# fp32 attention and max-of-three MoE: the first weight set as plain products, weight splits in pieces, h tiles loaded earlier

## The chip, the cores and the metric

One core of one Trainium2 chip. The metric is the device time of one execution in microseconds (us). The kernel before was timed in three runs: 632.27, 634.22 and 634.30, median 634.22.

## The reference

Attention over 4 batches, 8 heads, 576 positions, head size 64, with a bias per pair of positions from a small MLP; its output, laid out as 2304 tokens x 512, is multiplied by three weights, the largest of the three is kept, and a fourth weight projects back.

```python
scores = q @ k.T / sqrt(64) + bias(w1, b1, w2)      # 4 x 8 x 576 x 576
attn = exp(scores - max); attn = attn / (sum + 1e-9)
x = (attn @ v).transpose(0, 2, 1, 3).reshape(2304, 512)
h = np.maximum(np.maximum(x @ w1, x @ w2), x @ w3)  # w1..w3: 512 x 768
return h @ w_out                                    # w_out: 768 x 512
```

w1, w2, w3 and w_out arrive with 64 bits per element and are rounded to fp32 on the chip.

## The kernel before

Every fp32 product is made of three passes of TensorE on numbers split in two: a high part rounded by ScalarE (a cast to fp32r), and a low part that is the difference, by VectorE or GpSimd (`arith`, L417). The passes are high·high, high·low and low·high.

**Attention.** 16 units (a pair of heads, a batch) of 5 steps each; step n makes the scores (L254) of one 128-row tile, shifts them on VectorE (L264), takes the exponential on ScalarE (L276), normalises on GpSimd (L289), and for the step five back transposes on TensorE (L308, L317), copies those out (ScalarE L403/L404, VectorE L406) and multiplies with v (L347). `split_x` (L363) copies finished outputs into the twelve token blocks b12, b11, b21, b22 of the columns x = 0, 1, 2. `step` also advances the generators in `more`. One is `first()`: for weight sets 3 and 2 it converts the 64-bit words (`convert`, L483 to L495: one ScalarE and four VectorE instructions for 128x512 words, fetched by L477 into the one buffer `w64`) and parks the result in `w_d`; then it makes set 0 ready, converts w_out into `wo_d`, and converts set 1. The other is `combine(0)`: the splits and sums t1, t2, t3, t4 of the blocks of column 0.

**MoE.** Nine weight sets s (three 256-wide slices of d_ff, each for w1, w2, w3) and three columns x of 2 x 384 tokens give 27 groups. Each group is a Strassen-Winograd product of 2x2 blocks: seven products p1, p5, p6, p7, p2, p4, p3 of six 128x128x384 matmuls (L594 to L596), each into one of eight PSUM banks. ScalarE copies p1 and p5 out (m1 L612, m5 L614); VectorE adds p6 and p7 (mp) and makes c11, c21 and c12, each from one bank; GpSimd makes u and c22 from mp and m5 (L620); for w2 and w3, two VectorE instructions of 768 columns take the max into `ht`, the first right after c21, ahead of c12. The order of groups is (s, x) = (0,0), (1,0), (0,1), (1,1), (0,2), (1,2), then s = 2 to 8 with x inside. Column x + 1's `combine` runs inside the groups ahead of it; `weights` runs inside the others, one step per product: the sums of a set are four GpSimd instructions of 256 columns, its low parts (`split_w`) two of 768 and 1024 columns.

**Output.** After the last group the pool `xb` is released, h (stored to `h_d` by L636) is loaded back in six transfers of 3 x 128 tokens (L577, 1152 KB), split (ScalarE L584, VectorE), and multiplied with w_out in 18 tiles of 18 matmuls (L710 to L713); ScalarE copies a tile out (L714) and SP stores it (L715).

The engines each run their instructions in program order. All transfers are issued by SP, in program order too. The order in the program is thus that of the code: what stands between two products, and in which step a generator is advanced.

Of the kernel before, what the change touches and what calls it, by code (L numbers as in the profile page):

```python
# [9 lines left out]
F32 = mybir.dt.float32  # L10
# [9 lines left out]
def kernel(  # L20
# [45 lines left out]
    w_d = dram.tile([9, 128, 1024], F32, name="w_d")  # L66
# [352 lines left out]
    def combine(x, xa, fin):  # L419
        b12, b11, b21, b22 = raws[x]  # L420
        v, g = nc.vector, nc.gpsimd
        shape = [128, 2, TW]

        def tmp(n):
            return xa.tile(shape, F32, tag="tr", bufs=2, name=f"{n}_{x}")

        def high(n, src):
            h = fin.tile(shape, F32R, tag="xf", bufs=10 * (1 if x == 0 else NX - 1), name=f"{n}h_{x}")
            nc.scalar.copy(h, src)
            return h  # L430

        def low(eng, n, src, h, ring=False):
            o = (xa.tile(shape, F32R, tag="xr", bufs=4 * NX + 1, name=f"{n}l_{x}") if ring else
                 fin.tile(shape, F32R, tag="xf", bufs=10 * (1 if x == 0 else NX - 1), name=f"{n}l_{x}"))
            arith(eng, o, src, h)
            return h, o

        o = xs[x] = {}
        t1 = tmp("t1")
        arith(v, t1, b12, b11)  # L440
        yield
        h = high("t1", t1)
        yield
        o["t1"] = low(g, "t1", t1, h)
        h11 = high("b11", b11)
        yield
        if x == 0:
            yield
        t3 = tmp("t3")
        arith(v, t3, b22, b12)  # L450
        o["b11"] = low(g, "b11", b11, h11, True)
        h21 = high("b21", b21)
        yield
        t2 = tmp("t2")
        arith(v, t2, t3, b11, ALU.add)
        h = high("t3", t3)
        yield
        o["t3"] = low(v, "t3", t3, h, True)
        t4 = tmp("t4")
        arith(v, t4, b21, t2)  # L460
        h2 = high("t2", t2)
        yield
        o["b21"] = low(g, "b21", b21, h21, True)
        h22 = high("b22", b22)
        h4 = high("t4", t4)
        yield
        o["t2"] = low(v, "t2", t2, h2)
        o["b22"] = low(g, "b22", b22, h22, True)
        yield
        o["t4"] = low(v, "t4", t4, h4)  # L470
        yield

    def convert(pool, srcs, out, name):
        w = pool.tile([128, 512, 2], U32, tag="w64", bufs=1, name=f"w64{name}")
# [3 lines left out]
        for _ in range(2):  # L478
            yield
        a = pool.tile([128, 512], F32, tag="wa", bufs=1, name=f"wa{name}")  # L480
        t = pool.tile([128, 512], U32, tag="wt", bufs=1, name=f"wt{name}")
        high, low = w[:, :, 1], w[:, :, 0]
# [4 lines left out]
        nc.vector.tensor_scalar(out=t, in0=a.bitcast(U32), scalar1=3, scalar2=0x7FFFFFFF,  # L487
# [5 lines left out]
        if out is None:  # L493
            out = a.bitcast(U32)
        nc.vector.scalar_tensor_tensor(out=out, in0=high, scalar=signm, in1=t,  # L495
                                       op0=ALU.bitwise_and, op1=ALU.bitwise_or)
        yield a

    wf = {}
    PARK = 4  # L500

    def raw_w(wpool, s, parked=False):
        fp, i = divmod(s, 3)
        raw = wpool.tile([128, 1024], F32, tag="wr", bufs=2, name=f"wr{s}")
        wf[s] = raw
        if parked:
            nc.sync.dma_start(out=raw, in_=w_d[s])
            return
        m = (mw1, mw2, mw3)[i]
        for d in range(2):  # L510
            srcs = [m[256 * d:256 * d + 256, 256 * (2 * fp + b):256 * (2 * fp + b) + 256].rearrange(
                "(c p) f -> p c f", p=128) for b in range(2)]
            yield from convert(wpool, srcs, raw[:, 512 * d:512 * d + 512].bitcast(U32), f"{s}_{d}")

    def sum_w(wpool, s):
        raw = wf[s]
        sr = wpool.tile([128, 1024], F32, tag="wr", bufs=2, name=f"ws{s}")
        q = lambda t, n: t[:, 256 * n:256 * n + 256]
        wf[s] = (raw, sr)
        g = nc.gpsimd  # L520
        arith(g, q(sr, 0), q(raw, 0), q(raw, 2), ALU.add)
        yield
        arith(g, q(sr, 1), q(sr, 0), q(raw, 1))
        yield
        arith(g, q(sr, 2), q(raw, 1), q(raw, 0))
        yield
        arith(g, q(sr, 3), q(raw, 3), q(sr, 1))
        yield

    def split_w(pool, s):  # L530
        raw, sr = wf[s]
        hi = pool.tile([128, 1792], F32R, tag=f"wh{s % 2}", bufs=1, name=f"wh{s}")
        lo = pool.tile([128, 1792], F32R, tag=f"wl{s % 2}", bufs=1, name=f"wl{s}")
        wf[s] = (hi, lo)
        nc.scalar.copy(hi[:, 0:768], raw[:, 256:1024])
        arith(nc.gpsimd, lo[:, 0:768], raw[:, 256:1024], hi[:, 0:768])
        yield
        nc.scalar.copy(hi[:, 768:1792], sr)
        arith(nc.gpsimd, lo[:, 768:1792], sr, hi[:, 768:1792])
        yield  # L540
# [4 lines left out]
    def moe(pool, wpool, xa, xb):  # L545
        ht = pool.tile([128, NX, 5, TW], F32, name="ht", bufs=1)
        hd = h_d.rearrange("(f p) (t n) -> p f t n", p=128, t=2)
        wo = {}
        hs = {}
        hins = {}  # L550

        def load_wo(f):
# [10 lines left out]
            for _ in range(3):  # L563
                yield
# [282 lines left out]
```

## Time and profile before

| | |
|---|---|
| median of three runs | 634.22 us |
| the profiled execution | 636.11 us, of which the span is 634.1 us |
| TensorE (PE) busy | 592.1 us, 93% of the span |
| VectorE (DVE) busy | 425.1 us, 67% |
| ScalarE (ACT) busy | 343.9 us, 54% |
| GpSimd (POOL) busy | 326.5 us, 51% |
| DMA | 74.59 MB, mean 118 GB/s |

The busy times are sums over the whole span, over stages in which different engines do the work; matmuls are pipelined, so a busy TensorE may still run at half its clock. The span is what the trace shows from first to last instruction; the execution's own time is 2.0 us longer, and the profiled execution is 1.9 us above the median.

### The profile page before, as it was taken

To read this page: it belongs to the slowest core of one execution; us is meant where nothing else is said; L and a number is where in the kernel's file an instruction comes from. 1 tells how busy PE (TensorE), PEld (TensorE's weight loads), DVE (VectorE), ACT (ScalarE), POOL (GpSimd) and SP (SyncE) were. 2 spreads that over 40 slices of the span, in tenths; PEclk is the share of its full clock that TensorE was granted. 3 is DMA by queue.
4 is the path that set the end of the run, shared out by engine and by line. 5 is a ranking of instruction groups with operands and counts; after the bars stand their busy time and mean duration, and the time that the engine had idled before them with its cause. 6 is when DMAs were issued, how large, how long until landed. Compare 5 with 4: busy or idle time off the path is not lost.

```text
span 634.1 us, 12010 instructions
## 1 busy us (share of the span) xinstructions
PE 592.1 (93%) x4342; PEld 471.1 (74%) x4342; DVE 425.1 (67%) x902; ACT 343.9 (54%) x791; POOL 326.5 (51%) x285
## 2 busy tenths in 40 slices
PE   8999999999999999999896699999989999399998
PEld 4457666676766666666586699899989999278886
DVE  7995788788868778887738955755866667312221
ACT  7996988788898787887532422222312212123222
POOL 2605766666689555664568757546637545300000
PEclk9999999999999999999898899999989999689999
DMA  6897437533731384322110021321233113733431
GB/s 171 249 357 273 116 100 216 168 107 118 218 105 41 106 252 122 111 69 70 34 33 2 0 67 37 123 93 34 67 109 108 34 34 118 247 124 130 154 124 66
DMA packets 60202, 74.59 MB, mean 118 GB/s; under 512 B 22896, under 2 KB 41712, under 8 KB 60144
## 3 DMA queue, kind: packets, MB, share of 16 engines
q1 hardware_dynamic: 60000, 73.54, 36.8%
q8 instruction: 34, 0.56, 0.4%
q10 hardware_dynamic: 144, 0.29, 0.1%
q14 instruction: 24, 0.20, 0.1%
HBM read 48.51 MB, written 25.31 MB: 116 GB/s over the span
## 4 chain that ended last, share of the span: by engine, by line
PE 53%; DVE 10%; ACT 10%; POOL 9%; DMA 9%; issue 7%; SPq 1%; POOLq 0%; DVEq 0%; ACTq 0%
PE pv L347 10%; PE s L254 9%; PE tp L308 9%; PE o L710 4%; PE o L711 4%; PE o L713 4%; PE p L594 3%; PE p L595 3%; PE p L596 3%; DMA w<-in_moe_w_dram 3%; POOL q L620 3%; POOL wl L417 3%; DMA w64o<-in_moe_w_out_dram 2%; ACT bs L158 2%; DVE ht L417 2%
## 5 line engine op out<-in xcount | busy, mean ns | idle before, releaser
L289 POOL TENSOR_SCALAR e<-e,rc 128x576 f32<-128x576 f32 x144 | 108.8, 768 | 59.5 <-DVE rc L286 32.8
L276 ACT ACTIVATE e<-sn,nm 128x576 f32<-128x576 f32 x144 | 111.0, 774 | 34.2 <-DVE nm L264 32.7
L264 DVE CUSTOM_DVE_ANT_0 sn<-s,bias 128x576 f32<-128x576 f32 x128 | 91.8, 755 | 32.3 <-PE s L254 28.6
L308 PEld LDWEIGHTS tp<-ident,e 128*128 128x128 f32 x576 | 61.9, 142 | 42.1 <-issue 27.8
L308 PE MATMUL tp<-ident,e 128*128 128x128 f32 x576 | 83.0, 282 | 6.2 <-ACT et L403 5.6
L347 PE MATMUL pv<-et,vt 128*64 128x256 f32 (+1 forms) x496 | 74.6, 422 | 1.5 <-DVE xb L363 1.5
L223 POOL TENSOR_TENSOR kl<-kr,kh 128x640 fp32r<-128x640 f32 x16 | 35.6, 2227 | 57.5 <-ACT kh L222 57.4
L417 DVE TENSOR_TENSOR ht<-ht,q 128x768 f32<-128x768 f32 x36 | 38.6, 1073 | 37.9 <-POOL q L620 37.3
L417 DVE TENSOR_TENSOR hl<-hin,hh 128x768 fp32r<-128x768 f32 x18 | 17.1, 957 | 63.3 <-ACT hh L584 63.3
L406 DVE COPY et<-tp 128x512 f32<-128x512 f32 x64 | 43.7, 682 | 22.3 <-PE tp L308 22.3
L254 PE MATMUL s<-kh,qh 64*128 64x288 f32 (+1 forms) x288 | 57.2, 343 | 1.2 <-ACT bs L158 0.9
L710 PE MATMUL o<-woh,hh 128*128 128x512 f32 (+1 forms) x114 | 45.1, 399 | 11.0 <-ACT hh L584 11.0
L620 POOL TENSOR_TENSOR q<-mp,m 128x768 f32<-128x768 f32 x18 | 33.3, 1848 | 35.8 <-DVE mp L417 35.8
L403 ACT COPY et<-tp 128x512 f32<-128x512 f32 x80 | 45.9, 573 | 5.5 <-PE tp L308 5.3
L254 PE MATMUL s<-kl,qh 64*128 64x288 f32 (+1 forms) x288 | 48.6, 293 | 0.0
L347 PEld LDWEIGHTS pv<-et,vt 128*64 128x64 f32 x496 | 30.5, 136 | 24.0 <-issue 10.5
L254 PE MATMUL s<-kh,ql 64*128 64x288 f32 (+1 forms) x288 | 47.9, 290 | 0.0
L711 PE MATMUL o<-wol,hh 128*128 128x512 f32 (+1 forms) x114 | 44.4, 394 | 0.0
L138 PE MATMUL bp<-hid,w2s 128*32 128x79 f32 (+51 forms) x640 | 41.1, 391 | 2.3 <-DVE hid L117 1.9
L254 PEld LDWEIGHTS s<-kh,qh 64*128 64x128 f32 (+1 forms) x288 | 31.3, 184 | 13.2 <-issue 7.5
L714 ACT COPY ot<-o 128x512 f32<-128x512 f32 (+1 forms) x19 | 10.7, 564 | 55.7 <-PE o L713 55.7
L117 DVE TENSOR_SCALAR hid<-sm,bp 128x528 f32<-128x528 f32 (+17 forms) x108 | 40.7, 461 | 0.0
(143 smaller groups left out, 1490.5 us busy)
## 6 DMA issues: line engine op xcount, KB each, us to landing
bias_d<-bs SPq DMA_DIRECT2D x36, 295.5 KB, 5.7
bias<-bias_d SPq DMA_DIRECT2D x16, 576.0 KB, 4.2
w<-in_moe_w_dram SPq DMA_DIRECT2D x36, 256.0 KB, 3.2
h_d<-ht SPq DMA_DIRECT2D x18, 384.0 KB, 2.9
hin<-h_d SPq DMA_DIRECT2D x6, 1152.0 KB, 5.7
qr<-in_qd_dram SPq DMA_DIRECT2D x16, 320.0 KB, 3.7
kr<-in_kd_dram SPq DMA_DIRECT2D x16, 320.0 KB, 4.6
out_dram<-ot SPq DMA_DIRECT2D x17, 256.0 KB, 2.0
```

Of the source, the lines that this page charges most:

```text
L254: nc.tensor.matmul(ss[h][:, x, 0:HALF], lhsT=u[q][p, r], rhs=u[k][p, c:c + HALF], start=(j == 0), stop=(j == 2))
L264: nc.vector.tensor_tensor_reduce(out=sn.rearrange("p (a b) -> p a b", a=2), in0=st["s"][h][:, :, 0:HALF], in1=bt.rearrange("p (a b) -> p a ...
L276: nc.scalar.activation(st["e"][:, S * h:S * h + S], sn, ACTF.Exp, scale=-1.0, bias=nm, accum_out=st["sm"][:, h:h + 1])
L289: nc.gpsimd.tensor_scalar(out=e, in0=e, scalar1=rc[:, h:h + 1], scalar2=1.0, op0=ALU.mult, op1=ALU.mult)
L308: nc.tensor.transpose(tp[:, 128 * c:128 * c + 128], e2[:, k0:k0 + 128], ident)
L347: nc.tensor.matmul(pv[p], lhsT=w, rhs=x, start=(c == 0), stop=(c == NTQ))
L403: nc.scalar.copy(*tps[0])
L406: nc.vector.tensor_copy(*tps[1])
L417: eng.tensor_tensor(out=out, in0=f(a), in1=f(b), op=op)
L620: g.tensor_tensor(out=q[:, 1:3], in0=mp, in1=both, op=ALU.add)
L710: nc.tensor.matmul(po, lhsT=hh[:, f], rhs=woh[:, r], start=(f == 0), stop=False)
L711: nc.tensor.matmul(po, lhsT=hh[:, f], rhs=wol[:, r], start=False, stop=False)
```

## The change

1. **Set 0 is not Strassen.** The groups run as s = 0 to 8 with x inside. The three groups of set 0 are eight plain products (`plain`): four results of two products, copied from PSUM straight into `ht` by ScalarE. They need the split blocks, not the sums t1 to t4. For column 0 b12, b11 and t1 are split inside attention (`early_x`, `late_x`), t3 and t2 around the last `split_x`; for the columns 1 and 2 the splits stand in group 0 and the sums in groups 1 to 3.
2. **GpSimd in pieces, work at fixed places.** The low parts of a set are seven instructions of 256 columns, each put behind a given product; so are conversions, sums and reloads (a table `jobs`). The two max instructions stand behind c12, at the first two products of the group that follows, and the store of h behind the third. m1 and m5 have two buffers, not three.
3. **Conversion.** `w64` has two buffers, and each fetch is issued one conversion ahead; a conversion is five calls of its generator, not seven. The sums of the sets 3 and 2 are made and parked during attention too, and reloaded.
4. **Output.** h is loaded in 18 transfers of 128 tokens (384 KB). The first two are issued in the last group but one, three more in the last, and tile 0 is split there; no pool is released in between. w_out's parts are loaded in group 23 and split in the last three groups, GpSimd in pieces of 256 columns.

The core of the diff:

```diff
-    def combine(x, xa, fin):
-        b12, b11, b21, b22 = raws[x]
-        v, g = nc.vector, nc.gpsimd
-        shape = [128, 2, TW]
-
-        def tmp(n):
-            return xa.tile(shape, F32, tag="tr", bufs=2, name=f"{n}_{x}")
-
-        def high(n, src):
-            h = fin.tile(shape, F32R, tag="xf", bufs=10 * (1 if x == 0 else NX - 1), name=f"{n}h_{x}")
-            nc.scalar.copy(h, src)
-            return h
-
-        def low(eng, n, src, h, ring=False):
-            o = (xa.tile(shape, F32R, tag="xr", bufs=4 * NX + 1, name=f"{n}l_{x}") if ring else
-                 fin.tile(shape, F32R, tag="xf", bufs=10 * (1 if x == 0 else NX - 1), name=f"{n}l_{x}"))
-            arith(eng, o, src, h)
-            return h, o
-
-        o = xs[x] = {}
-        t1 = tmp("t1")
...
+    class Blocks:
+
+
+        def __init__(self, x, xa, fin):
+            self.x, self.xa, self.fin = x, xa, fin
+            self.src = dict(zip(("b12", "b11", "b21", "b22"), raws[x]))
+            self.hi = {}
+            xs[x] = self.out = {}
+
+        def home(self, n, k):
+            if n in F_OF:
+                return self.fin.tile(SHAPE, F32R, tag=f"f{self.x}_{F_OF[n] + k}", bufs=1, name=f"{n}{'hl'[k]}_{self.x}")
+            return self.xa.tile(SHAPE, F32R, tag=f"r{self.x}_{R_OF[n] + k}", bufs=1, name=f"{n}{'hl'[k]}_{self.x}")
+
+        def high(self, *names):
+            for n in names:
+                self.hi[n] = self.home(n, 0)
+                nc.scalar.copy(self.hi[n], self.src[n])
+
+        def low(self, n, eng=None):
+            o = self.home(n, 1)
+            arith(eng or nc.vector, o, self.src[n], self.hi[n])
+            self.out[n] = (self.hi[n], o)
+
+        def sum(self, n):
+            a, b, op = dict(t1=("b12", "b11", ALU.subtract), t3=("b22", "b12", ALU.subtract),
+                            t2=("t3", "b11", ALU.add), t4=("b21", "t2", ALU.subtract))[n]
+            self.src[n] = self.xa.tile(SHAPE, F32, tag="tr", bufs=2, name=f"{n}_{self.x}")
+            arith(nc.vector, self.src[n], self.src[a], self.src[b], op)
...
+    def fetch(pool, srcs, name):
+        w = pool.tile([128, 512, 2], U32, tag="w64", bufs=2, name=f"w64{name}")
         n = 512 // len(srcs)
         for x, src in enumerate(srcs):
             nc.sync.dma_start(out=w[:, n * x:n * x + n].rearrange("p (c f) t -> p c (f t)", c=src.shape[1]), in_=src)
-        for _ in range(2):
-            yield
+        return w
+
+    def convert(pool, w, out, name):
         a = pool.tile([128, 512], F32, tag="wa", bufs=1, name=f"wa{name}")
-        t = pool.tile([128, 512], U32, tag="wt", bufs=1, name=f"wt{name}")
-        high, low = w[:, :, 1], w[:, :, 0]
+        high, low, t = w[:, :, 1], w[:, :, 0], a.bitcast(U32)
...
+        def plain(x, slot):
+            for t in range(2):
+                for b in range(2):
+                    o = bank(f"c{b}{t}_{x}")[:, 0:TW]
+                    for d in range(2):
+                        n = (("b11", "b12"), ("b21", "b22"))[d][t]
+                        terms(o, wf[0], xs[x][n], 256 * (2 * d + b), d == 0, d == 1)
+                        if d:
+                            nc.scalar.copy(ht[:, x, 3 * b + t], o)
+                        slot()
...
-            if i:
-                arith(v, acc[:, 3:5], acc[:, 3:5], q[:, 3:5], ALU.max)
-            next(work, None)
+                after.append(lambda: arith(v, acc[:, 0:2], acc[:, 0:2], q[:, 0:2], ALU.max))
+                after.append(lambda: arith(v, acc[:, 3:5], acc[:, 3:5], q[:, 3:5], ALU.max))
+            if i == 2:
+                after.append(lambda: store(fp, x))
...
-        order = [(s, x) for x in range(NX) for s in (0, 1)] + [(s, x) for s in range(2, NSET) for x in range(NX)]
...
+        def lower_w(s, k):
+            raw, sr = made_w[s]
+            hi, lo = wf[s]
+            r = slice(256 * k, 256 * k + 256)
+            arith(g, lo[:, r], part(raw, k + 1) if k < 3 else part(sr, k - 3), hi[:, r])
...
+        for s in range(2, NSET):
+            n = 3 * s - 3
+            at(n, 0, F(raise_w, s, 0))
+            for k, y in enumerate((1, 4, 5)):
+                at(n, y, F(lower_w, s, k))
+            at(n, 4, F(raise_w, s, 1))
+            for k, y in enumerate((0, 1, 4, 5)):
+                at(n + 1, y, F(lower_w, s, 3 + k))
...
+        def load_h(k):
+            q, c = divmod(k, per)
+            x, t = divmod(q, 2)
+            hins[k] = home(k, 0, F32)
+            c0 = TW * x + 128 * c
+            nc.sync.dma_start(out=hins[k], in_=hd[:, :, t, c0:c0 + 128])
...
+        n = 3 * NSET - 2
+        at(n, 2, F(load_h, 0))
+        at(n, 3, F(load_h, 1))
+        at(n + 1, 2, F(load_h, 2), F(split_hi, 0))
+        at(n + 1, 3, F(load_h, 3))
+        at(n + 1, 4, F(split_lo, 0))
+        at(n + 1, 4, F(load_h, 4))
+
+        order = [(s, x) for s in range(NSET) for x in range(NX)]
...
+            def slot():
+                for f in after[:1]:
+                    after.pop(0)()
+                for f in jobs.pop((n, step[0]), ()):
+                    f()
+                step[0] += 1
+
+            (plain(x, slot) if s == 0 else group(s, x, slot))
...
+            if k + 5 < NK:
+                load_h(k + 5)
...
+            for _ in range(2):
+                yield
+            for s in PARK:
+                raw = raw_tile(wpool, 1)
+                for d in range(2):
+                    yield from conv(raw[:, 512 * d:512 * d + 512], f"{s}_{d}")
+                nc.sync.dma_start(out=w_d[s - PARK[1], 0], in_=raw)
+                sr = sum_tile(wpool, s)
+                yield from sum_w(raw, sr)
+                nc.sync.dma_start(out=w_d[s - PARK[1], 1], in_=sr)
...
+            if n >= 9 * NS - 1 and n % 3 == 0:
+                more.append(ex)
+            if n >= NSTEP - 2:
+                more.append(lx)
...
+        x0.sum("t3")
+        x0.high("t3")
+        x0.sum("t2")
+        x0.low("t3")
         at.split_x()
-        for w in (x0, w0):
-            for _ in w:
-                pass
+        x0.sum("t4")
+        x0.high("t2")
+        x0.low("t2", nc.gpsimd)
```

VectorE at the end of attention, before (t3, t2, t3l, t4 are sums and a low part of column 0; L406 copies transposes of the last unit; xb.._0 to xb.._2 are the token blocks):

```order
L417 TENSOR_TENSOR t2_0_4942<-t3_0_4920,xb11_0_908 128x768
L286 RECIPROCAL rc79_4946<-sm79_4913 128x1
L363 COPY xb21_1_913<-pv14_0_4862 128x192
L363 COPY xb21_2_917<-pv14_0_4862 128x64
L406 COPY et15_0_4951<-tp15_0_1_4957 128x4x128
L417 TENSOR_TENSOR t3l_0_4977<-t3_0_4920,t3h_0_4944 128x768
L417 TENSOR_TENSOR t4_0_4979<-xb21_0_909,t2_0_4942 128x768
L406 COPY et15_0_4951<-tp15_1_1_4988 128x4x128
L485 TENSOR_SCALAR wa1_1_4974<-wa1_1_4974 128x512
L363 COPY xb21_2_917<-pv14_256_4967 128x320
```

And after the change:

```order
L406 COPY et15_0_4965<-tp15_0_1_4971 128x4x128
L406 COPY et15_0_4965<-tp15_1_1_4993 128x4x128
L363 COPY xb21_2_917<-pv14_256_4981 128x320
L406 COPY et15_1_5008<-tp15_2_1_5014 128x4x128
L406 COPY et15_1_5008<-tp15_3_1_5034 128x4x128
L363 COPY xb22_1_914<-pv15_0_5024 128x192
L363 COPY xb22_2_918<-pv15_0_5024 128x64
L417 TENSOR_TENSOR t3_0_5073<-xb22_0_910,xb12_0_907 128x768
L417 TENSOR_TENSOR t2_0_5077<-t3_0_5073,xb11_0_908 128x768
L417 TENSOR_TENSOR t3l_0_5079<-t3_0_5073,t3h_0_5075 128x768
L363 COPY xb22_2_918<-pvlast_5062 128x320
L417 TENSOR_TENSOR t4_0_5082<-xb21_0_909,t2_0_5077 128x768
```

The sums stood among the copies of transposes; now they stand behind the last of those, and t3, t2 and t3l ahead of the copy of the last output (pvlast).

GpSimd from the sums of weight set 5 (ws5) to its last low part (wl5), before; ht and q are the u and c22 of groups:

```order
L417 TENSOR_TENSOR ws5_5970<-wr5_5829 128x256
L620 TENSOR_TENSOR ht_5107<-mp3_2_5943,m5_3_2_5942 128x768
L417 TENSOR_TENSOR ws5_5970<-ws5_5970,wr5_5829 128x256
L417 TENSOR_TENSOR ws5_5970<-wr5_5829 128x256
L417 TENSOR_TENSOR ws5_5970<-wr5_5829,ws5_5970 128x256
L417 TENSOR_TENSOR wl5_6021<-wr5_5829,wh5_6020 128x768
L417 TENSOR_TENSOR wl5_6021<-ws5_5970,wh5_6020 128x1024
L620 TENSOR_TENSOR q4_0_6008<-mp4_0_6011,m5_4_0_6010 128x768
L620 TENSOR_TENSOR q4_1_6086<-mp4_1_6089,m5_4_1_6088 128x768
```

And after the change, where L561 is the same u and c22:

```order
L417 TENSOR_TENSOR ws5_5974<-wr5_5695 128x256
L417 TENSOR_TENSOR ws5_5974<-ws5_5974,wr5_5695 128x256
L561 TENSOR_TENSOR ht_5099<-mp3_2_5965,m5_3_2_5964 128x768
L417 TENSOR_TENSOR ws5_5974<-wr5_5695 128x256
L417 TENSOR_TENSOR ws5_5974<-wr5_5695,ws5_5974 128x256
L417 TENSOR_TENSOR wl5_6048<-wr5_5695,wh5_6047 128x256
L561 TENSOR_TENSOR q4_0_6035<-mp4_0_6038,m5_4_0_6037 128x768
L417 TENSOR_TENSOR wl5_6048<-wr5_5695,wh5_6047 128x256 x2
L417 TENSOR_TENSOR wl5_6048<-ws5_5974,wh5_6047 128x256 x2
L561 TENSOR_TENSOR q4_1_6106<-mp4_1_6109,m5_4_1_6108 128x768
L417 TENSOR_TENSOR wl5_6048<-ws5_5974,wh5_6047 128x256 x2
```

The two long low parts stood ahead of group (4,0)'s q; now the pieces stand in pairs between the q of the groups.

SP's queue of transfers at the end of the MoE, from the first reload of w_out, before:

```order
L554 DMA wor0_6875<-wo_d_62 128x512
L554 DMA wor1_6914<-wo_d_62 128x512
L636 DMA h_d_61<-ht_5107 256x1x384 x2
L554 DMA wor2_6958<-wo_d_62 128x512
L554 DMA wor3_6996<-wo_d_62 128x512
L636 DMA h_d_61<-ht_5107 256x1x384 x2
L554 DMA wor4_7041<-wo_d_62 128x512
L554 DMA wor5_7082<-wo_d_62 128x512
L636 DMA h_d_61<-ht_5107 256x1x384 x2
L577 DMA hin0_7094<-h_d_61 128x6x384
L577 DMA hin1_7096<-h_d_61 128x6x384
L715 DMA out_0_dram<-ot0_7106 128x512
```

And after the change:

```order
L701 DMA wor0_6833<-wo_d_62 128x512 x2
L701 DMA wor2_6845<-wo_d_62 128x512 x2
L701 DMA wor4_6856<-wo_d_62 128x512 x2
L580 DMA h_d_61<-ht_5099 256x1x384 x2
L747 DMA hin0_7003<-h_d_61 128x6x128
L747 DMA hin1_7014<-h_d_61 128x6x128
L580 DMA h_d_61<-ht_5099 256x1x384 x2
L747 DMA hin2_7082<-h_d_61 128x6x128
L747 DMA hin3_7096<-h_d_61 128x6x128
L747 DMA hin4_7107<-h_d_61 128x6x128
L580 DMA h_d_61<-ht_5099 256x1x384 x2
L747 DMA hin5_7133<-h_d_61 128x6x128
```

The first loads of h stood behind the last store of h; now five of them stand ahead of it.

## Rows read from the trace of the kernel before

**Rows 1.** Windows: length; busy PE, PEld, DVE, ACT, POOL; granted clock, DMA share, GB/s.
```profile
49.80:319.77 269.97, 261.45 (x2216) 182.19 (x2216) 208.99 (x543) 216.82 (x581) 170.09 (x184) 0.99 0.42 127
319.77:386.19 66.42, 56.26 (x295) 54.73 (x295) 48.34 (x53) 21.50 (x34) 50.27 (x31) 0.92 0.08 24
386.19:497.82 111.63, 106.65 (x589) 103.00 (x589) 73.46 (x125) 26.63 (x47) 61.91 (x40) 0.98 0.26 86
497.82:541.55 43.73, 43.73 (x253) 43.57 (x252) 29.80 (x47) 9.93 (x19) 25.13 (x17) 1.00 0.22 69
552.70:634.10 81.40, 78.37 (x342) 63.69 (x342) 17.12 (x18) 23.12 (x36) 0.00 (x0) 0.96 0.35 122
```
**Rows 2.** Timeline of TensorE: the first matmul of two groups that follow one another.
```profile
505.10 0.33 PE L594 MATMUL p<-b11h,wh 128*128 128x384 f32 x1
...
512.39 0.33 PE L594 MATMUL p<-b11h,wh 128*128 128x384 f32 x1
```
**Rows 3.** Waits of TensorE in the MoE and the hole: us, times, longest.
```profile
PE p L594 <- DVE ht L417: 11.6, 6, 3.8
PE o L710 <- ACT hh L584: 11.0, 1, 11.0
```
**Rows 4.** Timeline in the second pair of groups: start, us, engine; idle before in brackets.
```profile
336.06 2.52 POOL L417 TENSOR_TENSOR b11l<-xb,b11h 128x768 fp32r<-128x768 f32 x1
336.95 2.44 DVE L417 TENSOR_TENSOR t<-xb,t 128x768 f32<-128x768 f32 x1
```
**Rows 5.** Timeline around set 5's low parts.
```profile
454.41 0.74 POOL L417 TENSOR_TENSOR ws<-ws,wr 128x256 f32<-128x256 f32 x1
454.49 1.47 DVE L417 TENSOR_TENSOR ht<-ht,q 128x768 f32<-128x768 f32 x1 [1.11 <-POOL q L620]
455.11 1.45 POOL L417 TENSOR_TENSOR ws<-wr 128x256 f32<-128x256 f32 x1
...
456.46 0.96 DVE L417 TENSOR_TENSOR ht<-ht,q 128x768 f32<-128x768 f32 x1
...
459.79 2.40 POOL L417 TENSOR_TENSOR wl<-ws,wh 128x1024 fp32r<-128x1024 f32 x1
462.15 1.86 POOL L620 TENSOR_TENSOR q<-mp,m 128x768 f32<-128x768 f32 x1
```
**Rows 6.** Waits of TensorE during attention.
```profile
PE tp L308 <- ACT et L403: 5.6, 7, 1.3
```
**Rows 7.** Timeline of TensorE (transposes) and ScalarE (a conversion) during attention.
```profile
117.05 0.63 PE L308 MATMUL tp<-ident,e 128*128 128x128 f32 x4 [0.89 <-ACT et L403]
...
208.42 0.67 ACT L483 ACTIVATE wao<-w64o 128x512 f32<-128x512 f32 x1 [1.55 <-DMA w64o<-in_moe_w_out_dram]
...
244.04 0.63 PE L308 MATMUL tp<-ident,e 128*128 128x128 f32 x4 [1.28 <-ACT et L403]
```
**Rows 8.** Timeline of TensorE and VectorE at attention's end.
```profile
300.71 2.58 DVE L417 TENSOR_TENSOR t<-xb,xb 128x768 f32<-128x768 f32 x1
...
303.14 0.27 PE L317 MATMUL lp<-ident,e 128*128 128x128 f32 x1
...
304.89 2.83 PE L347 MATMUL pv<-et,vt 128*64 128x320 f32 x12 [1.47 <-DVE xb L363]
...
309.21 0.27 PE L317 MATMUL lp<-ident,e 128*128 128x128 f32 x1
...
311.57 0.27 PE L317 MATMUL lp<-ident,e 128*128 128x128 f32 x1
```
**Rows 9.** The chain that ended last, around the hole ahead of the output.
```profile
545.13 6.67 DMA hin<-h_d
```
**Rows 10.** The page's DMA issues: KB each, median us to landing.
```profile
h_d<-ht SPq DMA_DIRECT2D x18, 384.0 KB, 2.9
```
**Rows 11.** Timeline of TensorE at the output's start.
```profile
552.70 0.79 PE L710 MATMUL o<-woh,hh 128*128 128x512 f32 x1 [10.99 <-ACT hh L584]
...
557.99 1.64 PE L713 MATMUL o<-woh,hl 128*128 128x512 f32 x6
```

## What the change should do

> **What bounds the kernel now.** I read the stages first [rows 1]. TensorE is busy nearly all of attention (261.45 of 269.97 us), of the late groups (43.73 of 43.73) and of the output. It has holes in three places: the first groups (56.26 of 66.42 busy, at a granted clock of 0.92), the middle groups (106.65 of 111.63), and the 11.15 us from 541.55 to 552.70, between the last window of groups and the output's. So TensorE bounds this kernel, and what counts is where something makes it wait or run at its lower clock.
>
> The price of a group with no wait is the distance of two first matmuls late in the MoE: 512.39 − 505.10 = 7.29 us [rows 2], that is 1.04 for each of seven products. 27 such groups are 196.8; the MoE takes 541.55 − 319.77 = 221.8. The loss of 25.0 splits by the same windows: the third window holds its six groups without loss; the second holds 14 groups in 111.63 where 14 × 7.29 = 102.1, so 9.5, or 0.68 a group; the rest, 15.5, falls to the first window.
>
> What makes TensorE wait there is VectorE, which comes late to empty PSUM banks [rows 3]: 11.6 us in 6 waits. Why it is late shows in the timeline: GpSimd's b11l and VectorE's t, both of 768 columns and both reading two SBUF tiles, take 2.52 and 2.44 us beside one another [rows 4]; the same VectorE form takes 0.96 alone, at 456.46 [rows 5]. Around 454.4 two GpSimd pieces of 256 columns and one VectorE max end 2.15 us after the first began (454.41 to 456.56); one after another they would be 0.74 + 0.74 + 0.96 = 2.44. So the two engines nearly take turns (2.15/2.44 = 0.88). And the wl of 2.40 us at 459.79 stands ahead of a group's u and c22 on GpSimd, which comes at 462.15 [rows 5]; VectorE's max and c12 wait behind that.
>
> At the end, the output's first matmul waits 10.99 us for hh [rows 3, 11], which waits for a 6.67 us load of h that is issued only after everything else [rows 9].
>
> **The change, part by part.** The terms come from the profiled execution: span 634.1 us, 636.11 with the 2.0 around it, which the change doesn't touch. The median of the three runs is 1.9 lower.
>
> *Hole ahead of the output: −11.15.* Tile 0's column is stored early in the last group but one, and its load stands behind that store. A store lands in 2.9 us [rows 10], a load takes at most today's 6.67 though it has a third of the bytes [rows 9], and from its end to the first matmul there lie 552.70 − 545.13 − 6.67 = 0.9 for ScalarE's split [rows 9, 11]. With the store issued behind the third product, some 3 us into its group, tile 0 is ready 3 + 2.9 + 6.67 + 0.9 = 13.5 us after that group began, 6.2 into the last, which takes 7.29. Tiles 1 to 4 are under way then. Cover gone: see R2.
>
> *Half clock at the output: −2.5.* The first twelve matmuls take 557.99 − 552.70 = 5.29 us [rows 11]; the other 330 take 81.40 − 5.29 = 76.1, or 0.231 each [rows 1], so twelve at that are 2.8. The granted clock falls after the long idle; with no idle the price goes.
>
> *Plain set 0 and the MoE: −17.3.* Three groups of eight products cost 3 × 8 × 1.04 = 25.0, 24 Strassen groups 24 × 7.29 = 175.0, together 199.95: 3.1 more work for TensorE than before. What stalls remain is the unknown. In the plain groups only ScalarE empties banks; TensorE needs of the others just the next column's low parts, 2 × 0.96 and 2 × 1.86 [rows 5], 5.6 us one after another in a group of 8.33. What VectorE and GpSimd lag behind is due in group 3. Lower bound: 0, no stall. Upper bound within this mechanism: the middle window's 0.68 a group in the 16 groups that have max and conversion, 10.9. Moving the max behind c12 takes the wait for u out of the way of bank release, and pieces of 0.74 replace a block of 1.86 and 2.40 ahead of u, so I take less than half of it: 4.5. That gives 221.8 − 199.95 − 4.5 = 17.3.
>
> *Conversion in attention: −4.0.* `tp` waits for ScalarE 5.6 us in 7 waits [rows 6]; ScalarE's conversion waits for its words, 1.55 us in the row shown, and the copies of transposes wait behind it [rows 7]. Four of the seven follow such a wait, 0.89 the first and 1.28 the last of them [rows 7], 4.0 together. With the fetch one conversion ahead the words are there. Bounds: 5.6 for all, and a loss of 1 if the eight more GpSimd sums and the early splits (some 0.74 to 1.86 each) make single steps late; GpSimd is busy 170 of 270 us there and nothing of it is on the path [rows 1].
>
> *Tail of attention: −1.6.* The sum t that takes 2.58 us at 300.71 delays the copies behind it, and TensorE idles 1.47 [rows 8]. That step lasts 309.21 − 303.14 = 6.07 us, the next 311.57 − 309.21 = 2.36 with six pv matmuls fewer (6 × 0.24, from 2.83 for twelve): 3.8 in all, so 2.3 back. But t3, t2 and t3l, about 0.96 each, now stand ahead of pvlast's copy on VectorE; they fit in its wait for pvlast but for about 0.7. Net −1.6; bounds −2.3 and 0.
>
> Fewer instructions elsewhere (weight sums reloaded, one buffer fewer for m1 and m5) I cost at nothing: reloads are hidden by whole groups, and m1 is read last by c11, two products before the next group's p1.
>
> Sum: −11.15 − 2.5 − 17.3 − 4.0 − 1.6 = −36.55. The profiled execution's 636.11 becomes 599.6, and the median 634.22 − 36.55 = **597.7 us**.
>
> **Rivals.**
>
> *R1, VectorE and GpSimd's turns bound the groups.* Pieces make nothing shorter; only the order changes. From group 0 to 8 GpSimd must do six u and c22 and six low parts of 1.86 and 21 + 4 pieces of 0.74 [rows 5]: 40.8 us. VectorE's two-tile work is 21 sums and low parts and 12 max of 0.96, 31.7, and three conversions, whose four instructions of 512 columns I put at two thirds of 0.96 each, 7.7: 39.4. Together 80.2, by the 0.88 above 70.6, while TensorE needs 3 × 8.33 + 6 × 7.29 = 68.7: hardly less. Later a set with max and conversion claims 13.7 + 10.9 = 24.6 in three groups, 21.6 by 0.88, against 21.9. If the turns are strict, the excess is 11.5 in the first nine groups and 2.7 in each of four later sets, S = 22.3 in place of 4.5: 597.7 + 17.8 = 616; where today's loss returns whole (15.5 + 16 × 0.68 = 26.4), 620. For it speaks what the two engines do to one another today [rows 4, 5]. Against: eight banks let VectorE lag almost a group before TensorE stops, and the cycles without max give time back. The Trainium skill ("SBUF — State Buffer", section "Who interferes with whom") speaks against this change: a VectorE instruction with two SBUF inputs and a GpSimd instruction that reads SBUF share a port pair, which whoever issues first holds for its whole instruction while the other fully blocks. This trace agrees, but for the 12% by which the shared stretch was shorter than the sum [rows 5]; by the rule the time is the strict one's.
>
> *R2, part of the hole stays.* Tile 0's load comes late by queueing behind w_out's reloads or stores. 5 us late plus the half clock's 2.5: about 605. For: a load of h took 6.67 us; against: the slack worked out above is 7.29 − 6.2 = 1.1 us even with that, more if fewer bytes take less.
>
> *R3, slower: h's loads feed the output too slowly.* Each transfer now moves pieces of 512 bytes, as many pieces as a transfer three times as large. If each takes 6.67 us as today [rows 9] and they queue behind one another, 18 × 6.67 = 120 us against 18 × 4.15 = 75 for the tiles: +45, about 642. It decides above 6.2 us a load (4.15 + 36.55/18). Against: two loads overlap today, and five stand ahead. The Trainium skill ("DMA: Bandwidth & Descriptors", "Specifications") gives 512 B as the least transfer for line rate, which these just reach; no run here shows it yet.
>
> *R4, the prefetch doesn't remove ScalarE's waits* (SP's queue, not the buffer, was late): +4, 602.
>
> **How the numbers follow.** Forecast 0.62, R1 0.20, R2 0.08, R4 0.04, R3 0.04, the rest 0.02. The forecast's own range is 588 (no stall, all bounds good) to 603 (S = 10.9). The range of 588 to 611 takes in the milder half of R1 (turns as loose as 0.88, lag returned in part) and leaves out the other half, R3 and the rest, 0.16. Within 0.3% is about what a measurement of this kernel can't tell from no change. Forecast, R1, R2 and R4 are all faster: 0.94; same 0.01; slower 0.05.
>
> **What would show it.** First matmul of the output within 1 us of the last of the groups, and its first tile at full clock (else R2). The three plain groups in about 25 us; later groups 7.3 to 7.6 each; a TensorE wait for VectorE's ht or q of many us in groups 3 to 8 or 12 to 20 would be R1, with VectorE and GpSimd instructions at 1.5 to 2.5 us beside each other. ScalarE's waits for w64 in attention gone (else R4). Loads of h under 4 us, and no wait of TensorE for hh in the output (else R3). A wait of tp for et in attention as large as before, or attention's end not 5 to 6 us earlier, would make those two terms wrong.

## Result and the profile after

The changed kernel takes 605.97 us (four runs, 605.92 to 606.03), the kernel before 633.75 in the same comparison: a ratio of 0.9565 (95% interval 0.9548 to 0.9583), so 4.4% faster. The forecast was 597.7, range 588 to 611. The profiled executions, 636.11 and 606.03 us, have spans of 634.1 and 604.2: 29.9 us to account for.

The stages of the changed kernel, columns as in [rows 1]; the fifth window is the output:

```profile
49.80:321.39 271.59, 259.74 (x2216) 182.33 (x2217) 205.46 (x541) 215.69 (x581) 172.77 (x195) 1.00 0.44 133
321.39:346.46 25.07, 25.07 (x145) 25.07 (x145) 20.10 (x13) 13.80 (x22) 16.70 (x9) 1.00 0.00 1
346.46:357.64 11.18, 9.52 (x43) 8.60 (x42) 8.43 (x8) 5.74 (x10) 4.25 (x4) 0.85 0.57 182
357.64:525.64 168.00, 168.00 (x967) 168.00 (x967) 140.53 (x195) 45.45 (x81) 121.10 (x105) 1.00 0.25 82
525.64:604.20 78.56, 75.58 (x343) 61.72 (x342) 19.36 (x22) 22.45 (x35) 0.00 (x0) 1.00 0.48 149
```

The three plain groups take 25.07 us, group 3 alone 11.18, the other 23 groups 168.00 with TensorE busy throughout (7.30 each). There is no window for the hole, since there is none. What grew is attention: 271.59 us where it took 269.97 [rows 1].

| term | forecast | measured |
|---|---|---|
| hole ahead of the output | −11.15 | −11.15 |
| half clock at the output (81.40 to 78.56) | −2.5 | −2.84 |
| groups (221.78 to 204.25) | −17.3 | −17.53 |
| tail of attention | −1.6 | −2.40 |
| conversion in attention | −4.0 | +4.02 |
| sum | −36.55 | −29.9 |

The last two terms part at one of L317's matmuls, at 298.27 us before and 302.29 after: up to it the change is 4.02 us late (0.44 of it already at the first such matmul, at 63.47 and 63.91), and from it to the first matmul of the MoE it takes 19.10 us where it took 21.50.

So four terms came out to within a microsecond and one came out with the wrong sign. TensorE's waits in attention show it:

```profile
PE pv L347 <- DVE xb L363: 8.1, 7, 1.7
...
PE tp L308 <- ACT et L403: 0.8, 1, 0.8
```

The wait that was to go has gone (5.6 us to 0.8, answering to [rows 6]), and another of 8.1 us in seven pieces has taken its place. The timeline of the first of them:

```profile
95.16 0.64 ACT L465 ACTIVATE wa<-w 128x512 f32<-128x512 f32 x1
...
95.84 0.43 DVE L467 TENSOR_SCALAR wa<-wa 128x512 f32<-128x512 f32 x1 [1.86 <-ACT wa L465]
96.18 0.15 DVE L286 RECIPROCAL rc<-sm 128x1 f32<-128x1 f32 x1
96.25 0.40 DVE L363 COPY xb<-pv 128x256 f32<-128x256 f32 x1
...
96.71 1.57 PE L347 MATMUL pv<-et,vt 128*64 128x320 f32 x10 [1.51 <-DVE xb L363]
```

Read from below: pv needs the PSUM bank that the copy to xb empties; the copy stands behind the conversion's second instruction on VectorE (L467); that one waits 1.86 us for the conversion's first, on ScalarE (L465), which itself stands behind two exponentials. Three of the seven waits look like this one; in three others the two last VectorE instructions of a conversion stand ahead of the copy, in one the two middle ones. All seven fall in the one step of five after the step with a single head (the fifth step of a unit takes the 64 rows that are left of both heads as one tile; the other four steps take a tile of each head).

Why there: `first()` is advanced seven times in five steps, and a conversion took seven advances before. It therefore met each step of the five with the same of its instructions, and in the written order of the kernel before none stands ahead of that copy in 14 of 15 such steps (the fifteenth has a sum of column 0: the 1.47 us of [rows 8]). With five advances a conversion drifts through the five steps; in the changed order 9 of the 15 have one or two, and seven of these nine are the seven waits.

In the MoE the waits were

```profile
PE p L524 <- ACT wh L628: 1.5, 1, 1.5
PE c L524 <- DVE xb L363: 1.2, 1, 1.2
PE p L526 <- POOL wl L417: 0.2, 1, 0.2
```

The 1.2 is the copy of pvlast behind t3, t2 and t3l. The others are all of group 3; after them some ten matmuls ran at half clock (0.32 us apart, not 0.174; the granted clock of that window is 0.85).

That half clock is not what makes group 3 long. In the kernel with two advances only in the step with one head (see the experiments) the same two waits come and the granted clock stays at 1.00, and the group takes 11.11 us all the same: TensorE then stands 1.48 us at its end, for ScalarE's copy of a plain result into `ht`.

```profile
339.44:350.55 11.11, 8.05 (x44) 7.02 (x43) 8.36 (x8) 5.75 (x10) 4.26 (x4) 1.00 0.55 184
...
350.55 0.45 PE L524 MATMUL p<-b11h,wh 128*128 128x384 f32 x1 [1.48 <-ACT ht L536]
```

In the changed kernel that copy comes just as late, behind a t2h that waits for VectorE's sum, and ends at 357.59, 0.05 us ahead of the first matmul of group 4; the half clock only hid the wait.

```profile
356.38 0.83 ACT L440 CAST t2h<-t 128x768 fp32r<-128x768 f32 x1 [2.25 <-DVE t L417]
357.12 0.47 ACT L536 COPY ht<-c 128x384 f32<-128x384 f32 x1
```

### The profile page after: what moved, and what is told of

The parts are those of the page before. It is cut to its first block, busy times and chain, and to the rows that moved or that the text cites. A ratio compares the mean times of both kernels' runs of the same rounds, so it can differ in the third digit from the quotient of the medians.

```text
span 604.2 us, 12112 instructions
## 1 busy us (share of the span) xinstructions
PE 583.6 (97%) x4360; PEld 469.6 (78%) x4360; DVE 438.3 (73%) x891; ACT 347.2 (57%) x800; POOL 330.1 (55%) x325
## 4 chain that ended last, share of the span: by engine, by line
PE 67%; DVE 7%; issue 2%; ACT 2%; POOL 1%; DMA 1%; DVEq 0%; ACTq 0%; POOLq 0%
PE p L526 10%; PE pv L347 10%; PE p L524 10%; PE p L525 10%; PE tp L308 8%; PE s L254 7%; PE o L795 4%; PE o L798 4%; PE o L796 4%; DVE t L417 1%; DVE sn L264 1%; PE lp L317 1%; DVE b12l L417 1%; DVE xb L363 1%; DMA w64o<-in_moe_w_out_dram 1%
## 5 line engine op out<-in xcount | busy, mean ns | idle before, releaser
L289 POOL TENSOR_SCALAR e<-e,rc 128x576 f32<-128x576 f32 x144 | 106.1, 749 | 71.9 <-DVE rc L286 41.3
L308 PE MATMUL tp<-ident,e 128*128 128x128 f32 x576 | 81.2, 281 | 1.8 <-ACT et L403 0.8
L553 ACT COPY m<-p 128x384 f32<-128x384 f32 x24 | 11.5, 481 | 90.2 <-PE p L526 40.9
L406 DVE COPY et<-tp 128x512 f32<-128x512 f32 x64 | 43.8, 685 | 22.5 <-PE tp L308 22.4
L561 POOL TENSOR_TENSOR q<-mp,m 128x768 f32<-128x768 f32 x18 | 33.3, 1848 | 33.3 <-DVE mp L417 32.3
L417 DVE TENSOR_TENSOR ht<-ht,q 128x768 f32<-128x768 f32 x36 | 45.5, 1303 | 0.0
L795 PE MATMUL o<-woh,hh 128*128 128x512 f32 (+1 forms) x114 | 43.4, 385 | 0.0
L796 PE MATMUL o<-wol,hh 128*128 128x512 f32 (+1 forms) x114 | 43.0, 381 | 0.0
```

The lines of the kernel that those rows point to most:

```text
L289: nc.gpsimd.tensor_scalar(out=e, in0=e, scalar1=rc[:, h:h + 1], scalar2=1.0, op0=ALU.mult, op1=ALU.mult)
L308: nc.tensor.transpose(tp[:, 128 * c:128 * c + 128], e2[:, k0:k0 + 128], ident)
L417: eng.tensor_tensor(out=out, in0=f(a), in1=f(b), op=op)
L795: nc.tensor.matmul(po, lhsT=hh[:, f], rhs=woh[:, r], start=(f == 0), stop=False)
L796: nc.tensor.matmul(po, lhsT=hh[:, f], rhs=wol[:, r], start=False, stop=False)
```

## Experiments

Each kernel is the changed one with the edit shown, unless another is named.

### Where the conversion stands in attention

Other steps for the second advance (none in the step in question):

```diff
-            if n >= 2 * NS and n % NS in (0, 4) and n < NSTEP:
+            if n % NS == 0:
+                more = []
+            elif n >= 2 * NS and n % NS in (1, 3, 4) and n < NSTEP:
                 more.append(w0)
```

> The changed kernel with the second advance of the weight conversion moved: none in every fifth step of attention (where it had two), two in three of the other four. Theory A (conversion instructions of VectorE stand ahead of the copy to xb in just those steps, and pv waits for that copy): the 8.1 us of pv's waits for xb go and attention ends about 8 us earlier, 598 us. Theory B (the added work in attention, eight more GpSimd sums and the early splits, is what costs): within 2 us of 606, the waits stand in other steps.

Measured 606.22 us (ratio 0.956, 0.9523 to 0.9597). Theory A as I put it falls. The wait for xb did go, to 1.3 us, but attention ended at the same time:

```profile
PE pv L347 <- PE s L254: 2.1, 3, 1.0
PE s L254 <- DVE nm L264: 2.0, 6, 0.7
PE pv L347 <- DVE xb L363: 1.3, 2, 0.9
PE pv L347 <- issue: 1.1, 1, 1.1
```

Four two-head steps, which had been clean, got 1.0 to 1.2 us longer each. The timeline of the first:

```profile
99.64 0.43 DVE L467 TENSOR_SCALAR wa<-wa 128x512 f32<-128x512 f32 x1 [2.19 <-ACT wa L465]
...
101.68 1.57 POOL L223 TENSOR_TENSOR ql<-qr,qh 128x640 fp32r<-128x640 f32 x1
...
102.00 1.53 DVE L469 TENSOR_SCALAR wa<-wa 128x512 uint32<-128x512 uint32 x1
...
103.53 0.53 DVE L363 COPY xb<-pv 128x128 f32<-128x128 f32 x2
...
104.16 1.08 PE L347 MATMUL pv<-et,vt 128*64 128x256 f32 x8 [0.95 <-PE s L254]
```

The pair of L465 and L467 now meets in another step, and VectorE waits 2.19 us for ScalarE there. Behind it stands the reciprocal that GpSimd needs; GpSimd's ql comes so late that the next step's L469 runs beside it, at 1.53 us in place of some 0.43 (the like of [rows 4]), and the copy and pv are late a step further on. What this pointed to was not the one copy, but any step with two heads that gets two advances; the next two runs test that.

Two advances only in the step with one head:

```diff
-            if n >= 2 * NS and n % NS in (0, 4) and n < NSTEP:
+            if n >= 2 * NS and n % NS == 4 and n < NSTEP:
```

> The changed kernel with two advances of the conversion only in the one step of five that has one head (n % 5 == 4); one in the others, so the step before pv's wait for xb has one, not two. Theory A2 (a step with two heads has no room on VectorE and ScalarE for two instructions of a conversion; moving the second advance to other two-head steps, as in the run before, moved the wait with it): the 8.1 us of waits go and come back nowhere, 598 to 600. Theory B (the added sums and early splits cost the time): 604 to 607.

Measured **600.36 us** (ratio 0.9475, 0.945 to 0.9501), 5.6 below the changed kernel, just above A2's range. Attention and the MoE's first matmul:

```profile
49.71:314.37 264.66, 259.48 (x2216) 182.10 (x2216) 210.04 (x541) 215.13 (x580) 171.75 (x195) 1.00 0.45 136
```

264.66 us: 5.31 less than before, where the forecast's two terms were 5.6 less. Of it 3.13 lie ahead of the L317 matmul at which the two terms part (at 295.05 here), where 4.0 were forecast, and 2.18 behind it, where 1.6 were. All the added sums and early splits are still in it, so theory B falls. This is the fastest kernel of the study; the other kernels near it (below) overlap with it in their single times.

The advances at the step's end, behind the copies:

```diff
-            for w in more:
-                next(w, None)
...
                     self.queue_pv(un, 128 * TS * g, w, *self.et)
+            for w in more:
+                next(w, None)
```

> The changed kernel with the same number of advances per step, but at the step's end, behind the copies to xb and of the transposes. Theory A1 (only the place ahead of the copies costs): the 8.1 us go, 598. Theory A2 (two in a two-head step cost wherever they stand): part of it, 2 to 5 us, comes back as waits for scores or shifts of the next step, 600 to 604. Theory B: 604 to 607.

Measured 601.16 us (0.9485, 0.9457 to 0.9513): A2's figure. The wait for xb is gone altogether, and the next step's shifts are late:

```profile
PE s L254 <- DVE nm L264: 3.4, 9, 0.7
```

The fetch issued later, on top of one double advance (600.36):

```diff
-                if todo:
-                    ahead.append(fetch(wpool, *todo.pop(0)))
-                yield from convert(wpool, ahead.pop(0), out.bitcast(U32), name)
+                for k, _ in enumerate(convert(wpool, ahead.pop(0), out.bitcast(U32), name)):
+                    if k == 3 and todo:
+                        ahead.append(fetch(wpool, *todo.pop(0)))
+                    yield
```

> The kernel with one double advance in five steps (e9_one_double, 600.4), and the fetch of a conversion's words issued within the conversion ahead of it, at its fourth of five calls, so about two calls ahead of their use as in the kernel before. Theory A (the fetch one whole conversion ahead is what freed ScalarE): waits of ScalarE for w come back, up to 4 us in TensorE's waits for et, 602 to 604. Theory B (two buffers, not the distance): no change, 600 to 601.

Measured 600.86 us (0.9462, 0.9433 to 0.9491): no change. ScalarE's waits for words, 6.6 us before, are 1.1:

```profile
ACT wa L465 <- DMA w<-in_moe_w_dram: 0.7, 1, 0.7
...
ACT wao L465 <- DMA w64o<-in_moe_w_out_dram: 0.4, 1, 0.4
```

So with the second buffer a lead of about two advances is enough here; the forecast's "one conversion ahead" was not what was needed.

### What frees the groups

Long low parts (sets 2 to 8), then the max where it stood, then both:

```diff
+                r, src = ((slice(0, 768), raw[:, 256:1024]), (slice(768, 1792), sr))[k]
+                arith(g, lo[:, r], src, hi[:, r])
...
             arith(v, c21, made("p4"), mp[:, 0], ALU.add)
+            if i:
+                arith(v, acc[:, 0:2], acc[:, 0:2], q[:, 0:2], ALU.max)
```

> The changed kernel with the low parts of sets 2 to 8 as two long GpSimd instructions (768 and 1024 columns), as before the change, in place of seven pieces. Theory A (a long block ahead of u and c22 is what made VectorE and so TensorE late before): up to 0.68 us in 14 groups comes back, 610 to 616. Theory B (the eight banks cover a block of 4.3 us once the max stands behind c12): within 1 us of 606.

Measured 609.49 us (0.961, 0.9567 to 0.9652), 3.5 more: just under theory A's range. The edit changes the place with the length: the two long parts stand behind the second and the fifth product of a set's first group, where the seven pieces are spread over two groups. This run doesn't tell the two apart.

> The changed kernel with the two max instructions where they stood before: the first between c21 and c12, the second right behind c12, both in their own group. Theory A (VectorE's wait for u, taken ahead of c12, keeps p3's bank and is the main loss of the groups before): 5 to 10 us come back, 611 to 616. Theory B (the pieces alone keep u early enough): within 1.5 us of 606.

Measured 607.33 us (0.9581, 0.9543 to 0.9619), 1.4 more, in the groups (205.67 us from first matmul to the output's, where the changed kernel takes 204.25).

> The changed kernel with both undone: low parts as two long GpSimd instructions and the max where they stood before. Alone they cost 3.5 and about 1.4 us (2.5 of it from group 8 on by the groups' starts). Theory A (each covers for the other: the before's 0.68 a group needs both): more than the sum, 8 to 12 us, 614 to 618. Theory B (independent): the sum, about 5 us, 611; what else the groups before lost would then be their order and the sums beside them.

Measured 615.28 us (0.9711, 0.9687 to 0.9734): 9.3 more, nearly twice the sum of the two. From the MoE's first matmul to the output's first it took 212.75 us where the changed kernel takes 204.25. The waits are of the kind that the kernel before had in these groups (first line): c12, which needs u, comes late with p3's bank.

```profile
PE p L594 <- DVE q L417: 2.2, 3, 1.8
...
PE p L524 <- DVE q L417: 5.4, 5, 1.7
...
PE p L524 <- DVE ht L417: 0.8, 2, 0.4
```

Either edit alone covers for most of the other: behind short pieces u comes early enough for a max in the old place; with the max out of the way the eight banks bridge most of a long block.

### The four microseconds of group 3

ScalarE in the changed kernel, the copies that group 3's p5 waits for:

```profile
347.31 0.83 ACT L440 CAST t1h<-t 128x768 fp32r<-128x768 f32 x1 [3.16 <-DVE t L417]
...
348.05 1.04 ACT L628 CAST wh<-ws 128x1024 fp32r<-128x1024 f32 x1
...
349.14 0.44 PE L524 MATMUL p<-t1h,wh 128*128 128x384 f32 x1 [1.46 <-ACT wh L628]
```

Set 1's high part stands behind column 2's t1h, which waits for a sum on VectorE.

```diff
-        at(1, 2, F(raise_w, 1, 0))
-        at(1, 7, F(raise_w, 1, 1))
+        at(0, 6, F(raise_w, 1, 0))
+        at(0, 7, F(raise_w, 1, 1))
```

> The changed kernel with ScalarE's two copies of set 1's high parts put into the first plain group, ahead of column 2's t1h. Group 3 takes 11.18 us where a group without a wait takes 7.29. Theory A (ScalarE's queue alone: the high part stands behind a copy that waits for VectorE's sum): 3.9 us less, 602.1. Theory B (GpSimd's low parts and VectorE's sums are late in any case): one to two of the four us come back as a wait for wl or t2l, 603 to 605.

Measured 605.32 us (0.9546, 0.9511 to 0.9582), 0.7 less, which neither theory gave. That wait went, and ScalarE's copies of plain results, behind the same sums, held TensorE for 2.2 us. Most of that was there before, hidden by the half clock: the wait that was taken away was not the one that set the group's length. Three more kernels, on top of one double advance (600.36), put t3, t2 and t3l behind the last copy to xb, which took 0.6 us off the wait for it (1.2 to 0.6), and moved the rest in turn: column 2's sums four products later; set 1's low parts ahead of t2l as well (at slots 0 to 4 of group 1); and those parts early without the later sums.

> e9_one_double with three more edits: set 1's high parts in the first plain group, column 2's sums and their splits four products later, t3, t2 and t3l behind the last copy to xb. Theory A (ScalarE's queue is what is late: its copies of plain results and of high parts stand behind copies that wait for VectorE's sums): of the 4 us that group 3 is too long and the wait for ht's copy, 3 to 4 come back, and 0.6 ahead of the MoE: 595.5 to 597. Theory B (VectorE and GpSimd are late in any order, and the shift carries the wait to group 5): 598.5 to 601.

Measured 601.11 us (0.9468, 0.9435 to 0.9501), at theory B's upper end; group 3 waits 3.5 us for wl, which stands behind a t2l that waits on GpSimd:

```profile
339.35 1.83 POOL L417 TENSOR_TENSOR t2l<-t,t2h 128x768 fp32r<-128x768 f32 x1 [5.80 <-ACT t2h L440]
341.14 1.43 POOL L417 TENSOR_TENSOR wl<-wr,wh 128x256 fp32r<-128x256 f32 x1
```

> e11_later_sums, with set 1's seven low parts on GpSimd ahead of column 1's t2l (which waits 5.8 us for ScalarE's copy of t2), in the second plain group. There TensorE waited 3.48 us for wl in group 3. Theory A (the queues' order is what is late, not the amount of work): that wait goes, group 3 takes 7.3 to 8 us, 596 to 597.5. Theory B (the amount, VectorE's and GpSimd's turns): the sums of the columns 1 and 2 come later by the pieces' time and a wait of 2 to 4 us stands in groups 3 to 5, 599 to 601.

Measured 600.65 us (0.9478, 0.9451 to 0.9505). That is theory B's figure. Group 3 is down to 8.13 us, but five of the next seven groups lost 0.6 to 1.7 each.

> The same with column 2's sums where the changed kernel has them. Theory A: ScalarE's copies of plain results stand behind its copies of column 2's sums, so the wait for ht's copy (2.2 us when only the high parts were early) is back, 598 to 600. Theory B: the sums, earlier, avoid the wait in groups 3 to 5 of its companion, 596 to 598.

Measured 601.88 us (0.9493, 0.9461 to 0.9525), above both theories; TensorE waits 4.9 us for ht's copies in and right behind group 3.

From the MoE's first to the output's first matmul these five orders took 204.25 (changed), 203.18, 206.03, 205.64 and 206.02 us. No order brought the four microseconds back: whatever was put first, something else of the same chain was late. That fits theory B, the amount of work that VectorE and GpSimd must do in turns up to group 8; that no order could do it isn't shown.

### Loads of h behind the groups

The five loads and tile 0's split moved behind the last group, in pieces of 128 tokens as in the changed kernel:

> The changed kernel with the loads of h and the split of tile 0 behind the last group, in pieces of 128 tokens. Theory A (the hole is the wait for one load, shorter by its size): 0.5 us of issue, about 3.9 for a load and 0.9 for the split, a hole of 5.5 to 6.5 us and 2.5 of half clock behind it, 614 to 615. Theory B (a load's time is set by its 768 pieces, not its bytes): a hole near 11 and 2.5 of half clock, 619.

Measured 617.41 us (0.9741, 0.9714 to 0.9767): 11.4 more, between the two. The end of the chain, with 0.56 us of c12, 1.75 of max and 0.5 of the store's issue ahead of it:

```profile
529.51 4.38 DMA hin<-h_d
533.91 0.84 ACT hh L751
534.80 0.79 PE o L793
```

TensorE waits 8.4 us, and the first twelve matmuls again take 5.5 (534.80 to 540.28). I had left out the wait for the last max and store, which no size of load shortens. A third of the bytes came in 4.38 us, not in 6.67 [rows 9]; of the 11.0 us of hole, 2.6 would have gone by smaller loads alone, and 8.4, with the half clock, by issuing them early.

## Why the prediction was right, and where it was off

That 605.97 lies in the range is in part luck. The forecast's own range ended at 603; what lies above was added for R1, and the time came out there because of the conversion in attention, which R1 has nothing to do with. The range's ends don't follow from the bounds either: with no stall, 5.6 for the conversion and 2.3 for the tail the sum gives 591, not 588, and S = 10.9 alone gives 604; with the conversion's loss of 1 and a tail of 0 beside it, 611.

**Hole and half clock** went as forecast, and the run without the early loads shows by how much. On the changed kernel the first output matmul follows the last of the groups after 0.17 us (525.47, 525.64), with the last max still to come on VectorE.

**Plain set 0 and the groups** came out at −17.53 for −17.3, with S = 4.30 (204.25 − 199.95) for the 4.5 that I took. The size was right by luck, for the place was not: I drew it from 0.68 us in each of 16 groups, and 3.9 of it stand in group 3 alone, behind VectorE's sums. The reason given for the later groups (the max behind c12, pieces instead of blocks) was shown by undoing it: 9.3 us for both. What the three plain groups earned by themselves was not tried; the part of the gain that lies in the first six groups, some 8 us, rests on the traces alone.

**R1** described what happens and not what it costs. VectorE and GpSimd do take nearly strict turns: in group 0 a pair ends every 2.53 us, where 0.96 and 1.86 [rows 5] add up to 2.82.

```profile
325.09 2.56 POOL L417 TENSOR_TENSOR b21l<-xb,b21h 128x768 fp32r<-128x768 f32 x1
325.86 2.61 DVE L417 TENSOR_TENSOR b12l<-xb,b12h 128x768 fp32r<-128x768 f32 x1
327.62 2.56 POOL L417 TENSOR_TENSOR b22l<-xb,b22h 128x768 fp32r<-128x768 f32 x1
328.39 2.60 DVE L417 TENSOR_TENSOR b11l<-xb,b11h 128x768 fp32r<-128x768 f32 x1
```

But in the 23 later groups VectorE was busy 140.53 of 168.00 us, turns included, and TensorE never waited. What the turns cost is at most the 4 us of group 3, not R1's 22.3. **R2, R3, R4** did not come: tile 0 was in time; loads of h land in 3.9 us (median) under the 4.15 of a tile, and ScalarE's waits for words in attention are gone.

```profile
hin<-h_d SPq DMA_DIRECT2D x18, 384.0 KB, 3.9
```

**Tail**: 2.4 for 1.6. t3, t2 and t3l cost the 0.6 that I had put at 0.7; the step at 303.14 gave back 3.17, not 2.3. I had misread it: the next step has four pv matmuls fewer, eight against twelve, not six, so by that reckoning 2.8; and the step before the change ran at a granted clock of 0.72, after it at 1.00.

**Conversion in attention: the step that failed.** I costed the change from seven advances to five at nothing and let the loss from this part end at 1 us. The waits I counted did go. But the conversion's place in the five steps is itself a schedule: seven advances against seven kept VectorE's instructions out of the steps that had no room for them. The new wait cost 8.1 us where 4.8 had gone. With the advances put where there is room, attention gives the 5.3 us that were forecast as 5.6, and the kernel takes 600.36 us in all. The experiments show that the place of the conversion's instructions costs this time. That the place moved because of five calls for seven is read from the order of VectorE's instructions; the changed kernel with seven calls was not run, and the sums of sets 3 and 2 add calls of their own.

## What to carry to other kernels

When side work is fed into a loop in instalments, its period against the loop's is part of the schedule. Before shortening a generator by a call, list what stands ahead of the loop's tightest copy in each step, before and after. A wait on an engine that runs in order is priced with what is queued behind it: here a 0.43 us instruction cost TensorE 1.5 us. And two edits that protect the same wait are to be undone together as well as singly, or each looks worth less than it is: 3.5 and 1.4 us singly, 9.3 together.

## What I had not expected of the hardware

An instruction of VectorE with one input can wait for GpSimd too: the conversion's TENSOR_SCALAR (L467), 0.43 us alone, took 1.92 beside GpSimd's u and c22 in the changed kernel, as L469 took 1.53 beside ql above.

```profile
388.87 1.85 POOL L561 TENSOR_TENSOR q<-mp,m 128x768 f32<-128x768 f32 x1 [2.12 <-DVE mp L417]
389.08 1.92 DVE L467 TENSOR_SCALAR wa<-wa 128x512 f32<-128x512 f32 x1
```

The Trainium skill ("SBUF — State Buffer", "Who interferes with whom") says that tensor_scalar can contend with GpSimd when it runs in a two-port mode. No row here names the mode; the times agree: GpSimd's instruction ends at 390.72 and VectorE's at 391.00, 0.28 us later. My claims for R1 had counted the conversions for their own time, but not that they queue for the whole of a GpSimd instruction.
